# Hash attention before an MLP mixer: scores on four 32-row tiles instead of two 64-row tiles

## The chip, the core and the metric

The kernel runs on one core of one Trainium2 chip. The metric is the device time of one execution in microseconds (us). TensorE is called PE, its weight loads PEld, VectorE DVE, ScalarE ACT, GpSimd POOL; SP is the sync engine, which here only issues DMAs.

## What is computed

Attention over 4 batches of 8 heads, 768 positions, 64 columns a head, with a hash mask, and then an MLP mixer on its output (the change doesn't touch the mixer). The attention, cut to its core:

```python
q_bits = (np.einsum('bhsd,dk->bhsk', q, proj) > 0)     # 6 bits a position
k_bits = (np.einsum('bhsd,dk->bhsk', k, proj) > 0)
mask = q_bucket[:, :, :, None] == k_bucket[:, :, None, :]   # all 6 bits equal
scores = np.where(mask, scale * (q @ k.T), -1e9)
attn = exp(scores - max) ; attn = attn / (attn.sum(-1) + 1e-09)
out = attn @ v
```

The kernel adds the mask as a product of bits: each bit is +0.5 or -0.5, those of k are scaled by 2^20, and a seventh row cancels the sum where all six agree; elsewhere the exponential becomes 0. A tiny constant, 2^-70, stands in each sum and in the sum of v, so that a row with no match stays finite.

## The kernel before, in words

The 32 heads are worked in 16 pairs. A pair `n` has q and k as one tile `qk` of 128 rows: the 64 columns of head 0 above those of head 1, fp32, 768 positions each. Its work:

- **Scores** (`Half.scores`, line 356). The 768 query positions go in two halves of 384, the 768 keys in six blocks of 128, so there are 12 blocks. For a block, the two heads' products run as two matmuls of 64 rows, on the upper and lower 64 rows of the array, into two PSUM banks (one bank pair, tag `sc`). The mask follows as two bf16 matmuls of 64 rows from `bits` (7 rows are used). An fp32 matmul appears in the trace as two PE instructions.
- **Exponential** (line 363): one ACT instruction a block, 128 x 768, into a tile `e` (12 buffers).
- **Sum over keys**: DVE adds a half's six `e` into `esd` (lines 391, 395, 398); a product with ones (line 434) sums over the 128 rows, ACT takes Ln and Exp (438, 439) and DVE and ACT refine and spread it (`newton`). This is done for the pair before, one pair late.
- **Hash of the next pair** (`hashes`, line 301): four matmuls of 32 output rows; DVE makes bits (305), ACT scales them (309), and eight DMAs from SP copy them to their rows in `bits` (line 314), of which there are two, one for even and one for odd pairs.
- **Product with v** (`weigh`, line 410): 24 matmuls a half, each of 32 output rows; ACT adds the sum of v and writes `num` (416); DVE multiplies by the reciprocal (459). The sum of v came from a load of v transposed (`vT`, line 282) and an ACT activation with accumulation (289).
- Beside it DVE and ACT convert 64-bit weights (lines 177 to 206), and every second pair DVE transposes finished blocks and SP writes them out (`bounce`, 238).

PSUM has eight banks: three bank pairs `sc` (which also serve the hash and the second `acc`), one bank `sm` for sums and one bank `acc`. All engines work in the order in which the code is written (a manual schedule); SP issues its DMAs in one queue in that order. The lines that set the order of a pair:

```python
for now in halves:
    now.scores()
    ...
if before:
    before.sums()
if 0 < n < len(pairs) - 1:
    hashes(n + 1)
halves[1].add_last()
...
load_qk(n + 2)
...
halves[0].weigh()
...
halves[1].weigh()
```

Of the kernel before, what the change touches and what calls it, by code (L numbers as in the profile page):

```python
# [48 lines left out]
def kernel(  # L49
    ctx: ExitStack,  # L50
    tc: tile.TileContext,
    qk: bass.AP,
    v: bass.AP,
    vT: bass.AP,
# [8 lines left out]
    nc = tc.nc  # L63
# [14 lines left out]
    assert S == 6 * P and DM == 512 and NB <= 8 and DTOK % P == 0 and DCH % P == 0  # L78
# [14 lines left out]
    projs = const.tile([P, P + 32], F32, name="projs")  # L93
    nc.scalar.dma_start(out=projs, in_=proj_pair)
    projwide, projblk = projs[:, :P], projs[:, P:]
    ones = const.tile([P, D], F32, name="ones")
# [17 lines left out]
    nc.gpsimd.memset(bitscale, BIG)  # L114
    for j in range(4):
        if j % 2 == 0:
            nc.gpsimd.memset(bitscale[32 * j : 32 * j + 32], 1.0)
        else:
            for i in range(2):
                cancel(bitscale, 32 * j + 16 * i + NB)  # L120
# [137 lines left out]
    def attention(pool, psum, W1, W2, x0):  # L258
        bitrows = [pool.tile([P, 2, S], BF16, name=f"bits{n}", tag=f"bits{n}", bufs=1) for n in range(2)]
        loaded = {}  # L260

        def load_qk(n):
            if n >= len(pairs):
                return
            b, hp = pairs[n]
            t = pool.tile([P, 2, S], F32, name="qk", tag="qk", bufs=3)
            if n:
                nc.sync.dma_start(out=t, in_=qk[b, hp])
            else:
                for i in (1, 0):  # L270
                    nc.sync.dma_start(out=t[:, i, :HALF], in_=qk[b, hp, :, i, :HALF])
                nc.sync.dma_start(out=t[:, :, HALF:], in_=qk[b, hp, :, :, HALF:])
            loaded[n] = [t, None, None, None]

        def load_v(n):
            if n >= len(pairs):
                return
            b, hp = pairs[n]
            vn = pool.tile([P, 2, NR, D], F32, name="vn", tag="vn", bufs=2)
            nc.sync.dma_start(out=vn, in_=v[b, hp])  # L280
            vt = pool.tile([P, S], F32, name="vt", tag="vt", bufs=2)
            nc.sync.dma_start(out=vt, in_=vT[b, hp])
            loaded[n][1:3] = vn, vt

        def add_values(n):

            vt = loaded[n][2]
            vsum = pool.tile([P, 1], F32, name="vsum", tag="vsum", bufs=4)
            nc.scalar.activation(vt, vt, ACT.Copy, scale=-EPS, accum_out=vsum)
            loaded[n][3] = vsum  # L290

        def hashes(n):

            g = pool.tile([P, HALF], BF16, name="g", tag="g", bufs=2)
            if n == 1:
                ps = psum.tile([P, 512], F32, name="hp", tag="sm", bufs=1)
            else:
                ps = psum.tile([P, 2, 512], F32, name="hp", tag="sc", bufs=3)[:, 0]
            for j in range(4):
                sl = slice(HALF * (j // 2), HALF * (j // 2) + HALF)  # L300
                nc.tensor.matmul(  # L301
                    ps[32 * j : 32 * j + 32, :HALF], projblk, loaded[n][0][:, j % 2, sl],
                    start=True, stop=True,
                )
            nc.vector.tensor_scalar(g, ps[:, :HALF], 0.0, 0.5, op0=ALU.is_gt, op1=ALU.subtract)
            if n == 1:
                nc.vector.tensor_scalar(g, g, bitscale, None, op0=ALU.mult)
            else:
                nc.scalar.mul(g, g, bitscale)
            for j in range(4):  # L310
                sl = slice(HALF * (j // 2), HALF * (j // 2) + HALF)
                for i in range(2):
                    at = 32 * j + 16 * i
                    nc.sync.dma_start(
                        out=bitrows[n % 2][D * i : D * i + NB + 1, j % 2, sl], in_=g[at : at + NB + 1],
                    )

        def first_hashes(half):

            sl = slice(HALF * half, HALF * half + HALF)  # L320
            ps = psum.tile([P, 512], F32, name="hw", tag="sm" if half else "acc", bufs=1)[:, :HALF]
            for i in range(2):
                for which in (1, 0):
                    at = D * i + 32 * (1 - which)
                    nc.tensor.matmul(  # L325
                        ps[at : at + 32], projwide[:, D * i : D * i + 32], loaded[0][0][:, which, sl],
                        start=True, stop=True,
                    )
            q, k = (bitrows[0][:, which, sl] for which in range(2))
            nc.vector.tensor_scalar(k, ps, 0.0, 0.5, op0=ALU.is_gt, op1=ALU.subtract)  # L330
            if half:
                nc.vector.tensor_scalar(k, k, widescale, None, op0=ALU.mult)
            else:
                nc.scalar.mul(k, k, widescale)
            for i in range(2):
                at = D * i
                nc.vector.tensor_scalar(
                    q[at : at + 32], ps[at + 32 : at + 64], 0.0, 0.5, op0=ALU.is_gt, op1=ALU.subtract,
                )

        class Half:
# [5 lines left out]
            def scores(self):  # L347

                qkt, bits = loaded[self.n][0], bitrows[self.n % 2]
                qs = slice(HALF * self.half, HALF * self.half + HALF)  # L350
                first = self.n == self.half == 0
# [9 lines left out]
                def exponential(sc):  # L361
                    e = pool.tile([P, 2, HALF], F32, name="e", tag="e", bufs=12)
                    nc.scalar.activation(e, sc[:, :, :HALF], ACT.Exp, scale=SCALE)  # L363
                    self.es.append(e)

# [3 lines left out]
                for c in range(NR):  # L369
                    sc = psum.tile([P, 2, 512], F32, name="sc", tag="sc", bufs=3)  # L370
                    if c == self.half == 0 and not first:
                        product(sc, bits, c, True)
                        product(sc, qkt, c, False)
                        exponential(sc)
                        continue
# [4 lines left out]
                    for block, ps in waiting:  # L380
                        product(ps, bits, block, False)
                        exponential(ps)
# [17 lines left out]
            def weigh(self):  # L400

                _, vn, _, vsum = loaded[self.n]
                if self.half:
                    acc = psum.tile([P, 2, 512], F32, name="acc", tag="sc", bufs=3)[:, 0, :HALF]
                else:
                    acc = psum.tile([P, 512], F32, name="acc", tag="acc", bufs=1)[:, :HALF]
                for c, e in enumerate(self.es):
# [6 lines left out]
                if self.half == 0:  # L414
                    nums[self.n] = pool.tile([P, 2, HALF], F32, name="num", tag="num", bufs=2)
                nc.scalar.activation(  # L416
                    nums[self.n][:, self.half], acc, ACT.Identity, scale=-1.0, bias=vsum,
                )

        nums = {}  # L420

        class Quotients:
# [5 lines left out]
            def sums(self):  # L428

                ps = psum.tile([P, 512], F32, name="sums", tag="sm", bufs=1)[:, :HALF]  # L430
                for i in range(2):
                    for h in range(2):
                        at = 32 * (2 * i + h)
                        nc.tensor.matmul(  # L434
                            ps[at : at + 32], ones[:, :32], self.halves[h].d[:, i], start=True, stop=True,
                        )
# [5 lines left out]
            def newton(self):  # L442

                ps, near = self.ps, self.near
                t = pool.tile([P, HALF], F32, name="t", tag="t", bufs=1)
                rec = self.rec = pool.tile([P, 2, HALF], F32, name="rec", tag="rec", bufs=2)
                nc.vector.tensor_tensor(t, ps, near, op=ALU.mult)
# [19 lines left out]
        nc.vector.memset(bitrows[0][:, 0], 0.0)  # L467
        nc.gpsimd.memset(bitrows[1], 0.0)
        load_qk(1)

        idle = psum.tile([P, 512], F32, name="idle", tag="sm", bufs=1)
        for _ in range(6):
            zeros = bitrows[0][:, 0]
            nc.tensor.matmul(idle[:D, :HALF], zeros[:, :D], zeros[:, :HALF], start=True, stop=True)  # L474
# [9 lines left out]
        for n in range(len(pairs)):  # L484
# [3 lines left out]
            for now in halves:  # L488
                now.scores()
                if n == 0 and now.half:  # L490
                    hashes(1)
                now.add()
                if now.half == 0:
                    now.add_last()
            if before:
                before.sums()
            if 0 < n < len(pairs) - 1:
                hashes(n + 1)
# [4 lines left out]
            add_values(n)  # L503
# [4 lines left out]
            halves[0].weigh()  # L508
            if n + 1 == len(pairs):
                before.divide()  # L510
                before = Quotients(halves)
                before.sums()
                before.newton()
                weights.turnover()
                halves[1].weigh()
# [4 lines left out]
            halves[1].weigh()  # L520
# [1249 lines left out]
```

## Time and profile before

| | |
|---|---|
| median of 3 runs | 787.82 us (787.6 to 788.1) |
| span of the profiled execution | 786.3 us, 1.5 below the median |
| busy: PE, PEld, DVE, ACT, POOL | 99%, 61%, 85%, 62%, 7% |
| granted PE clock | 1.00 throughout |
| attention | from the start to about 310 us |

The span runs from the first to the last instruction of one profiled execution. In a timeline each row has the start and the length in us, engine, line, operation, the tile written and those read, shapes, and how many instructions were merged; in brackets, how long the engine was idle before and what released it. The names are those of the code, without buffer numbers.

### The profile page before, as it was taken

How to read it: one execution, taken by the hardware profiler on the slowest of the kernel's cores; microseconds unless marked ns; L12 is line 12 of the kernel's file. 1: busy time of each engine (PE TensorE's matmuls, PEld its weight loads, DVE VectorE, ACT ScalarE, POOL GpSimd, SP SyncE). 2: the span in 40 equal slices, each digit the busy share in tenths (PEclk: the TensorE clock that was granted, in tenths of full speed). 3: DMA queues.
4: the chain of work that ended last, by engine and by line, in shares of the span. 5: the costliest groups of instructions: out<-in, count | busy, mean ns of one | idle time of the engine just before them, and what ended most of it. 6: DMA issues, size and time to landing. Idle time of an engine off the chain costs nothing.

```text
span 786.3 us, 12638 instructions
## 1 busy us (share of the span) xinstructions
PE 780.1 (99%) x4751; PEld 483.5 (61%) x4751; DVE 669.5 (85%) x918; ACT 484.7 (62%) x837; POOL 54.2 (7%) x77
## 2 busy tenths in 40 slices
PE   9999999999999999999999999999999999999997
PEld 4444444444444444455544448888887888886886
DVE  5989898989897677999787888999899799889884
ACT  6688888888888887233323225656774667665331
POOL 1000000000000000011120110120000122000001
PEclk9999999999999999999999999999999999999999
DMA  4435353537352425786487897797776784850565
GB/s 165 163 125 163 125 164 125 163 124 244 125 166 88 127 95 180 200 259 133 90 253 263 276 392 276 226 295 204 233 223 203 249 251 126 242 171 2 184 170 133
DMA packets 102529, 145.38 MB, mean 185 GB/s; under 512 B 30200, under 2 KB 72640, under 8 KB 102464
## 3 DMA queue, kind: packets, MB, share of 16 engines
q1 hardware_dynamic: 94448, 119.68, 46.5%
q0 software_dynamic: 7728, 24.64, 13.5%
q8 instruction: 38, 0.62, 0.3%
q10 hardware_dynamic: 288, 0.21, 0.1%
q14 instruction: 27, 0.22, 0.1%
HBM read 101.53 MB, written 35.52 MB: 174 GB/s over the span
## 4 chain that ended last, share of the span: by engine, by line
PE 99%; DVE 0%; issue 0%; DVEq 0%
PE b L785 50%; PE sc L356 20%; PE acc L410 16%; PE t L658 5%; PE t L698 5%; PE sums L434 2%; PE hp L301 1%; PE hw L325 0%; PE idle L474 0%; DVE second L1030 0%; DVE bits L467 0%; DVE ones L97 0%; PE b L1614 0%; DVEq L1765 0%
## 5 line engine op out<-in xcount | busy, mean ns | idle before, releaser
L363 ACT ACTIVATE e<-sc 128x768 f32<-128x768 f32 x192 | 154.5, 810 | 7.0 <-PE sc L356 6.6
L356 PE MATMUL sc<-qk 64*128 64x384 f32 x768 | 153.7, 486 | 0.0
L785 PE MATMUL b<-R,second 128*128 128x256 f32 (+1 forms) x522 | 131.9, 409 | 0.0
L410 PE MATMUL acc<-e,vn 128*32 128x384 f32 x1536 | 127.0, 486 | 0.0
L785 PEld LDWEIGHTS b<-R,second 128*128 128x128 f32 x522 | 99.0, 190 | 28.7 <-issue 16.5
L395 DVE TENSOR_TENSOR esd<-esd,e 128x768 f32<-128x768 f32 x96 | 92.0, 958 | 10.4 <-ACT e L363 0.5
L410 PEld LDWEIGHTS acc<-e,vn 128*32 128x32 f32 x1536 | 49.9, 110 | 73.9 <-issue 73.5
L356 PEld LDWEIGHTS sc<-qk 64*128 64x128 f32 x768 | 68.7, 189 | 42.3 <-issue 38.1
L791 ACT COPY c<-b 128x256 f32<-128x256 f32 (+1 forms) x96 | 40.3, 426 | 79.4 <-PE b L785 68.2
L356 PE MATMUL sc<-bits 64*128 64x384 bf16 x384 | 62.5, 323 | 0.0
L785 PE MATMUL b<-XT,WC 128*128 128x256 f32 (+1 forms) x208 | 61.0, 428 | 0.0
L391 DVE SCALAR_TENSOR_TENSOR esd<-e 128x768 f32<-128x768 f32 x32 | 30.6, 955 | 23.4 <-ACT e L363 23.3
L785 PEld LDWEIGHTS b<-XT,WC 128*128 128x128 f32 x208 | 39.5, 190 | 15.4 <-issue 10.5
L785 PE MATMUL b<-XT,SW 128*128 128x256 f32 (+1 forms) x164 | 47.0, 410 | 0.0
L658 PE MATMUL t<-x,W 128*128 128x512 f32 x96 | 41.8, 593 | 0.0
L356 PEld LDWEIGHTS <-bits 64*128 64x128 bf16 x384 | 18.7, 94 | 33.1 <-issue 9.9
L416 ACT ACTIVATE num<-acc,vsum 128x384 f32<-128x384 f32 x32 | 18.6, 581 | 29.8 <-PE acc L410 29.4
L785 PEld LDWEIGHTS b<-XT,SW 128*128 128x128 f32 x164 | 31.1, 190 | 9.4 <-issue 4.1
L718 POOL DMA_DIRECT2D XT<-second x8 | 9.8, 1228 | 385.6 <-DVE second L717 363.4
L455 ACT COPY rec<-rec 32x384 f32<-32x384 f32 x64 | 32.7, 510 | 5.0 <-DVE rec L449 4.2
L398 DVE TENSOR_TENSOR esd<-esd,e 128x768 f32<-128x768 f32 x32 | 30.5, 954 | 1.9
L658 PEld LDWEIGHTS t<-x,W 128*128 128x128 f32 x96 | 18.2, 190 | 22.7 <-issue 21.3
(246 smaller groups left out, 1282.2 us busy)
## 6 DMA issues: line engine op xcount, KB each, us to landing
second<-left SPq DMA_DIRECT2D x20, 768.0 KB
raw<-in_moe_w_ch SPq DMA_DIRECT2D x16, 768.0 KB
qk<-in_qk SPq DMA_DIRECT2D x15, 768.0 KB
second<-left SPq DMA_DIRECT2D x18, 576.0 KB
seen<-in_qk POOLq DMA_DIRECT2D x21, 384.0 KB, 4.6
WC<-hidden_left SPq DMA_DIRECT2D x18, 448.0 KB
vn<-in_v SPq DMA_DIRECT2D x16, 384.0 KB
vt<-in_vT SPq DMA_DIRECT2D x16, 384.0 KB
```

The source lines that it names most:

```text
L356: nc.tensor.matmul(sc[:, i, :HALF], t[rows, 1, P * c : P * c + P], t[rows, 0, qs], start=start, stop=not start,)
L363: nc.scalar.activation(e, sc[:, :, :HALF], ACT.Exp, scale=SCALE)
L391: nc.vector.scalar_tensor_tensor(self.d, es[0], NR * EPS, es[1], op0=ALU.add, op1=ALU.add,)
L395: nc.vector.tensor_tensor(self.d, self.d, e, op=ALU.add)
L398: nc.vector.tensor_tensor(self.d, self.d, self.es[-1], op=ALU.add)
L410: nc.tensor.matmul(acc[D * i + d : D * i + d + 32], vn[:, i, c, d : d + 32], e[:, i], start=(c == 0), stop=(c == NR - 1),)
L416: nc.scalar.activation(nums[self.n][:, self.half], acc, ACT.Identity, scale=-1.0, bias=vsum,)
L455: nc.scalar.copy(rec[other : other + 32, h], rec[at : at + 32, h])
L658: nc.tensor.matmul(ps, W1[:, r, P * j : P * j + P], x[:, r], start=(r == 0), stop=(r == NR - 1),)
L698: nc.tensor.matmul(ps[at], left, right, start=start, stop=True, skip_group_check=True,)
L785: nc.tensor.matmul(ps, left(k), right(k), start=start and k == ks[0], stop=stop and k == ks[-1], skip_group_check=True,)
L791: nc.scalar.copy(c, ps)
```

## The change

Every score product is cut into two parts of 32 rows. The host lays q and k out anew (`in_qk_rows`): rows 0 to 31 and 32 to 63 serve the even key blocks of head 0 and head 1, rows 64 to 95 and 96 to 127 the odd blocks. A row group holds its 32 columns of q for all 768 positions and of k for its three blocks (384 positions), once for each of two parts, so the tile has 2 x (768 + 384) columns. `bits` has the same four row groups. Block `j` runs on the two row groups of its parity, and its second part is written in the order behind the mask product of block `j + 1`.

```diff
+        def scores(halves):
+            qkt, bits = parts(loaded[halves[0].n][0]), bitrows[halves[0].n % 2]
+            blocks = [(now, c) for now in halves for c in range(NR)]
...
+            def product(j, part):
...
+                q, k = (bits[:, :S], bits[:, S:]) if part < 0 else qkt[part]
+                qs = slice(HALF * now.half, HALF * now.half + HALF)
+                ks = slice(P * (c // 2), P * (c // 2) + P)
+                for i in range(2):
+                    at = 32 * (2 * (c % 2) + i)
+                    nc.tensor.matmul(
+                        made[j][:, i, :HALF], k[at : at + 32, ks], q[at : at + 32, qs],
+                        start=part < 0, stop=part == 1,
+                    )
+            product(0, -1)
+            for j, (now, _) in enumerate(blocks):
+                product(j, 0)
+                product(j + 1, -1)
+                product(j, 1)
+                now.exponential(made[j])
```

The hash takes six matmuls, DVE's operation becomes two (one for k on 64 rows and 192 columns, one for q on 64 rows and 384), ACT scales k's part alone, and the bits go to four row groups:

```diff
-            for j in range(4):
-                sl = slice(HALF * (j // 2), HALF * (j // 2) + HALF)
-                for i in range(2):
-                    at = 32 * j + 16 * i
+            for j in range(2):
+                for i in range(4):
+                    at, of = 32 * i, 32 * j + 8 * i
                     nc.sync.dma_start(
-                        out=bitrows[n % 2][D * i : D * i + NB + 1, j % 2, sl], in_=g[at : at + NB + 1],
+                        out=to[at : at + NB + 1, S:][:, quarter[j]], in_=g[of : of + NB + 1, : HALF // 2],
                     )
+            for j in range(2):
+                for i in range(4):
+                    at, of = 32 * i, D + 32 * j + 8 * (i % 2)
+                    nc.sync.dma_start(out=to[at : at + NB + 1, half[j]], in_=g[of : of + NB + 1])
```

All eight banks become four bank pairs in one rotation (`bank_pair`): twelve for the blocks of a pair, one that sums and hash share, one for both halves of the product with v. The exponentials go to one tile `exps` with a column of -2^-70 behind each 384, and the first half's product with v takes that column too, which gives the sum of v; the load of `vT` and its activation go.

```diff
+        exps = pool.tile([P, 2 * NR, 2, HALF + 1], F32, name="exps", tag="exps", bufs=1)
...
+        def bank_pair(name):
+            return psum.tile([P, 2, 512], F32, name=name, tag="sc", bufs=4)
...
+                columns = HALF if self.half else HALF + 1
+                acc = to[:, self.half, :columns]
...
+                    vsum = loaded[self.n][2] = pool.tile([P, 1], F32, name="vsum", tag="vsum", bufs=2)
+                    nc.scalar.copy(vsum, acc[:, HALF:])
...
-            nc.scalar.activation(vt, vt, ACT.Copy, scale=-EPS, accum_out=vsum)
```

The first pair keeps its 64-row products (`first_scores`), with its bits in a place borrowed from `x0`. In a later pair both halves' scores come first, and then the hash, the additions in the order of before, and the sums.

Where the instructions stand now. On SP, in one pair between two loads of v, before (`bits` are the copies of hash bits, `qk` the load for the pair after next, `raw` a weight, `bounced` finished output):

```order
L280 DMA vn<-in_v 128x768
L282 DMA vt<-in_vT 128x768
L314 DMA bits_136<-g 7x384 x8
L268 DMA qk<-in_qk 128x1536
L169 DMA raw<-in_moe_w_ch 128x1536
L238 DMA bounced_104<-stage 32x24x64 x4
```

and in the changed kernel:

```order
L288 DMA vn<-in_v 128x768
L319 DMA bits_147<-g 7x192 x8
L325 DMA bits_147<-g 7x384 x8
L270 DMA qk<-in_qk_rows 128x2304
L166 DMA raw<-in_moe_w_ch 128x1536
L235 DMA bounced_115<-stage 32x24x64 x4
```

Eight copies of bits became sixteen, first the eight of k with 192 columns, then the eight of q with 384, and the load of `qk` stands behind all of them.

On PE, where a pair ends with its product with v and the next pair's first blocks begin, before (`acc` is the product with v, `sc` a block; a bf16 weight load has its own row):

```order
L410 MATMUL acc<-e,vn 32x384 x48
L356 LDWEIGHTS bits_136
L356 MATMUL sc<-bits_136 128x384
L356 LDWEIGHTS bits_136
L356 MATMUL sc<-bits_136 128x384
L356 MATMUL sc<-qk 128x384 x4
```

and now, with what an instruction waits for in brackets (a DMAHW name is the landing of a DMA, here copies of bits):

```order
L442 LDWEIGHTS bits_147 [waits DMAHW0_49]
L442 MATMUL sc<-bits_147 128x384 [waits PE_49]
L442 LDWEIGHTS bits_147 [waits DMAHW1_49]
L442 MATMUL sc<-bits_147 128x384 [waits DMAHW1_49]
L442 MATMUL sc<-qk 128x384 x2
L442 LDWEIGHTS bits_147 [waits DMAHW2_49]
L442 MATMUL sc<-bits_147 128x384 [waits PE_49]
L442 LDWEIGHTS bits_147 [waits DMAHW3_49]
L442 MATMUL sc<-bits_147 128x384 [waits DMAHW3_49]
L442 MATMUL sc<-qk 128x384 x4
```

The second block's mask product, with its own two waits for bits, stands between the two halves of the first block's product. Before, the first block's mask and whole product followed each other.

More of the change, by code (lines that the diff above doesn't have):

```diff
@@ L305, in hashes @@
[L305 to L312, printed above, removed]
-                    at = 32 * j + 16 * i
+                nc.scalar.mul(g[:D, : HALF // 2], g[:D, : HALF // 2], bitscale[:D])
@@ L369, in scores @@
                 for c in range(NR):
[L370 to L375, printed above, removed]
+                    sc = bank_pair("sc")
                     product(sc, qkt, c, True)
@@ L398, in add_last, with weigh @@
                 nc.vector.tensor_tensor(self.d, self.d, self.es[-1], op=ALU.add)
[L400 to L407, printed above, removed]
+            def weigh(self, to):
+                _, vn, vsum = loaded[self.n]
+                columns = HALF if self.half else HALF + 1
+                acc = to[:, self.half, :columns]
+                for c in range(NR):
+                    e = exps[:, NR * self.half + c, :, :columns]
                     for i in range(2):
@@ L519, in attention @@
             weights.turnover()
[L520 removed]
+            halves[1].weigh(acc)
             if n and n % 2 == 0:
```

172 lines of the change are left out of this document (106 added, 66 removed).

## The prediction, made before the changed kernel ran

> **What bounds the kernel now.** I read the page first, then the busy time by stretches, then the timeline of one head pair, engine by engine. Of the page, the span, the first engine row and the chain of work that ended last:
>
> ```profile
> span 786.3 us, 12638 instructions
> PE 780.1 (99%) x4751; PEld 483.5 (61%) x4751; DVE 669.5 (85%) x918; ACT 484.7 (62%) x837; POOL 54.2 (7%) x77
> PE 99%; DVE 0%; issue 0%; DVEq 0%
> PE b L785 50%; PE sc L356 20%; PE acc L410 16%; PE t L658 5%; PE t L698 5%; PE sums L434 2%; PE hp L301 1%; PE hw L325 0%; PE idle L474 0%; DVE second L1030 0%; DVE bits L467 0%; DVE ones L97 0%; PE b L1614 0%; DVEq L1765 0%
> ```
>
> PE is busy 780.1 of 786.3 us. The change touches only the attention, lines 356, 410, 434 and 301: some 39% of the chain, the first 310 us. Its second pair begins, one in the middle runs, and the last one begins and makes its last block (timeline, PE; start and length in us, last the number of merged instructions):
>
> ```profile
> 26.02 0.34 PE L356 MATMUL sc<-bits 64*128 64x384 bf16 x2
> ...
> 109.80 0.33 PE L356 MATMUL sc<-bits 64*128 64x384 bf16 x2
> 109.96 0.81 PE L356 MATMUL sc<-qk 64*128 64x384 f32 x4
> 110.60 0.33 PE L356 MATMUL sc<-bits 64*128 64x384 bf16 x2
> ...
> 111.67 0.85 PE L434 MATMUL sums<-esd,ones 128*32 128x384 f32 x8
> 112.33 0.83 PE L301 MATMUL hp<-qk,projs 128*32 128x384 f32 x8
> 112.98 7.92 PE L410 MATMUL acc<-e,vn 128*32 128x384 f32 x96
> 120.84 0.34 PE L356 MATMUL sc<-bits 64*128 64x384 bf16 x2
> ...
> 291.51 0.34 PE L356 MATMUL sc<-bits 64*128 64x384 bf16 x2
> ...
> 301.04 0.33 PE L356 MATMUL sc<-bits 64*128 64x384 bf16 x2
> ```
>
> From 26.02 to 291.51 are 14 pairs: 18.96 us each. One pair is 12 score blocks of 0.81 us (109.80 to 110.60), sums 0.66, hash 0.65, and the product with v, 112.98 to 120.84, 7.86. ScalarE in the same pair, all engines' busy time in it (the row of sums of windows from 101.87 to 120.84), VectorE and the SP queue:
>
> ```profile
> 102.90 9.68 ACT L363 ACTIVATE e<-sc 128x768 f32<-128x768 f32 x12 [0.32 <-PE sc L356]
> 112.59 0.49 ACT L438 ACTIVATE near<-sums 128x384 f32<-128x384 f32 x1
> 113.11 0.53 ACT L439 ACTIVATE near<-near 128x384 f32<-128x384 f32 x1
> 114.31 0.62 ACT L309 ACTIVATE g<-g,bitscale 128x384 bf16<-128x384 bf16 x1 [0.68 <-DVE g L305]
> 114.84 0.83 ACT L289 ACTIVATE vt<-vt 128x768 f32<-128x768 f32 x1
> 121.87 0.81 ACT L363 ACTIVATE e<-sc 128x768 f32<-128x768 f32 x1 [0.32 <-PE sc L356]
> ```
>
> ```profile
> sum 18.97, PE 18.97 PEld 8.88 DVE 17.79 ACT 16.17 POOL 0.00; mean PE 6.32 PEld 2.96 DVE 5.93 ACT 5.39 POOL 0.00
> ```
>
> ```profile
> 104.55 0.96 DVE L391 SCALAR_TENSOR_TENSOR esd<-e 128x768 f32<-128x768 f32 x1 [0.34 <-ACT e L363]
> ...
> 113.73 0.55 DVE L305 TENSOR_SCALAR g<-hp 128x384 bf16<-128x384 f32 x1
> ```
>
> ```profile
> 104.23 4.67 SPq L238 DMA_DIRECT2D bounced<-stage  x4
> ...
> 114.96 5.91 SPq L314 DMA_DIRECT2D bits<-g  x8
> 120.91 0.44 SPq L268 DMA_DIRECT2D qk<-in_qk  x1
> 121.40 0.42 SPq L169 DMA_DIRECT2D raw<-in_moe_w_ch  x1
> ```
>
> Call E the start of a pair's first exponential; PE began that pair 1.03 us before (120.84 against 121.87). The exponentials run without a gap at 0.807 us, as fast as PE makes blocks. The next pair's hash bits are ready late: VectorE takes them at E + 10.83 (113.73 - 102.90), behind nine additions of exponentials; ScalarE scales them; SP issues the first copy of bits at G = E + 12.06. The first block of the next pair needs copies 0 to 3. The eight copies start 0.746 us apart ((5.91 - 0.69) / 7, with 0.689 us for each by this view of line 314):
>
> ```profile
> L314 SPq DMA_DIRECT2D bits<-g x120: 688/689/938, 19.4 to 291.0; - x120
> ```
>
> How soon they land is in the moved bytes, here 40 slices of 0.25 us from 112 to 122 us:
>
> ```profile
> GB/s 307 418 442 320 111 61 0 0 0 0 0 33 0 0 0 0 0 22 0 0 22 0 0 22 0 0 87 0 0 22 0 0 22 0 0 22 0 0 22 49
> ```
>
> The eight marks of 22 are the eight copies, the first in 116.25 to 116.50: at most 1.5 us after its issue began, and I take 1.3. Copy 3 lands at G + 3.5 = E + 15.6; the next scores start at E + 17.94. So the bits have 2.4 us to spare now, no wait shows, and PE alone sets the 18.96.
>
> **The change, part by part.** *Scores.* The fp32 product of a block is cut in two halves of 32 rows, and the mask product shrinks to 32 rows. A matmul of 384 columns takes as long with 64 rows as with 128:
>
> ```profile
> L356 PE MATMUL sc<-qk 64*128 64x384 f32 x768 | 153.7, 486 | 0.0
> L410 PE MATMUL acc<-e,vn 128*32 128x384 f32 x1536 | 127.0, 486 | 0.0
> L356 PE MATMUL sc<-bits 64*128 64x384 bf16 x384 | 62.5, 323 | 0.0
> ```
>
> so fewer rows save nothing; only work side by side does. The 486 and 323 hold some 0.16 us of pipeline (a block of two fp32 passes and a mask is 0.807, that is 0.323 + 0.323 + 0.161). A block on its own rows will take 4 x 0.323 + 0.161 = 1.45 us, and with even and odd blocks side by side PE makes one per 0.73 us, 0.08 less than now: 1.0 us a pair at best. That tiles on all four row groups run side by side no row of before shows. Bounds: 0.73, or 1.45 where they don't overlap. I take 0.73, because the two row tiles of now (four instructions of 0.81 us together, each listed with 0.486) and the four column tiles (96 of 0.486 in 7.92) do overlap. Yet almost nothing of it reaches the end. ScalarE still needs 0.807 a block, and with four bank pairs exponential 7 must end (E + 6.46) before block 11 starts, which then takes 1.45: PE leaves the scores at E + 8.0 instead of E + 8.7 (last mask product at 301.04 of a pair that began at 291.51). And the first block, alone on its rows, is ready 1.45 + 0.25 = 1.7 us after PE begins the pair, not 1.03. Minus 0.7 and plus 0.7: with nothing else in the way a round would be 8.0 + 0.66 + 0.65 + 7.86 + 0.1 for the change of tiles + 1.7 = 18.97 us, against 18.96.
>
> *Sum of v.* One more column in 24 matmuls, and a copy of 128x1 on ScalarE, for the activation of 0.83 us on line 289. It stands where ScalarE waits for PE anyway: nothing. The loads stay at 1,536 KB (qk grows by 384 KB, vT goes).
>
> *Hash bits.* This is where I see the price. VectorE's operation becomes two; ScalarE's takes 64x192, which no row shows. Bounds for the first part of VectorE 0.3 to 0.55 us, for ScalarE's 0.2 to 0.62; I take 0.35 and 0.42, some two thirds of now for half the columns, so G comes at E + 11.65. PE's hash work keeps 0.65 (its longest column tile still has 384 columns in all), and it ends before VectorE has made its nine additions. Then **SP issues 16 copies where it issued 8**, the eight of k first, the eight of q after. The first block of the next pair reads copies 0, 1, 8 and 9; the second 2, 3, 10 and 11. In PE's order the second block's mask product stands ahead of the first block's second half, and an instruction that waits on PE holds all behind it: nothing of the next pair is finished before copy 11 has landed.
>
> A copy of 7 rows of 384 bytes is not in the trace. Nearest rows: 0.746 for 7 rows of 768 bytes on the same queue; 0.42 to 0.44 for loads of 128 rows (121.40 and 120.91), for which bytes make no difference (6,144 a row); 1.17 for the writes of line 238 (4.67 / 4). I take 0.746, the same rows and queue. For the landing, bounds from the start of the issue are its own 0.69 us and the 2.9 of the projection load below (0.84 to 3.72); I take the 1.3 of the copies' own row.
>
> ```profile
> 0.84 0.39 ACTq L94 DMA_DIRECT2D projs<-in_proj_pair  x1
> 3.72 0.18 PEld L325 LDWEIGHTS hw<-qk,projs 128*32 128x32 f32 x2 [0.76 <-DMA projs<-in_proj_pair]
> ```
>
> Copy 11 begins at G + 11 x 0.746 = G + 8.2 and lands at G + 9.5. Then block 0's second half, 0.65, and the pipeline with a semaphore, 0.25: the next E is G + 10.4. **The new round is 11.65 + 10.4 = 22.05 us**, 3.09 over 18.96. PE would be ready at E + 17.3 and waits some 3 us a pair (copy 9 lands at E + 19.7, copy 11 at E + 21.2). VectorE (17.8 us of work, 0.35 more now), ScalarE (16.2, 1.0 less) and SP (11.9 for copies, 4.7 + 0.4 + 0.4 and a load of v) all fit in 22. The load of qk, queued behind the copies, now begins at G + 11.9 and is first read at G + 19.2; at 400 GB/s (the row of bytes) 1,152 KB need 3 us. Copies 12 and 13, which block 6 reads, land by G + 11; its bank pair is free at G + 12.8.
>
> *Sum.* The first copies go out at 19.4 now and some 0.3 later then, so the second pair's E moves from 27.05 to 30.1: +3.1. Fourteen rounds of +3.09: +43.3. The last pair's scores end 0.7 earlier: -0.7. Together **+45.7**, on the profiled 786.3 us of span 832.0; the median stands 1.5 us over the span, so about **834 us**.
>
> **Rivals.** *The bits arrive in time.* The round is then the 18.97 us worked out above, and with the shorter end of the last pair the time **787 us**: not slower, within 0.2%. For it speaks that SP has room: sixteen copies are 11.9 us of a round of 19. It decides at the step of one copy: copy 11 at E + 11.65 + 11s + 1.3 must be there when the first half of block 0 ends, at E + 18.1, so s must be 0.46 us or less, for k and q alike. Against it: the q copies have the very shape that takes 0.746. If PE's lead were worth more than I give it (12 x 0.08 = 1.0 us a pair), it would end at 773. *Only k's copies are cheap*, 0.47 us (0.42 and a gap of 0.05): copy 11 begins at 8 x 0.47 + 3 x 0.746 = 6.0, the round is 19.85, 15 x 0.9 = +13: **801 us**, still slower. *The tiles don't run side by side*, so that the change doesn't do what it says: if PE starts matmuls strictly in order, a matmul's second pass begins before the next matmul's first, and a block costs 4 x 0.323 = 1.29 us. Exponential 10 then ends at E + 13.7 (10 x 1.29 + 0.81), and with the last addition (0.96), the hash and its scaling G moves to E + 15.6; the round is 26: 15 x 7, with a last pair longer by some 5: **898 us**. Against it: by that order a step of four matmuls on line 410 would take 1.29 too, and 12 steps take 7.86, 0.655 each. [...]
>
> **How the numbers follow.** Forecast 834, chance 0.73: its own range, with the landing between its bounds (-0.6 and +1.6 us in 15 rounds), is 825 to 858. Cheap k copies, 801: 0.08. In time, 773 to 790: 0.12, of which 0.06 is faster by over 0.2%, 0.05 within 0.2% (about what a measurement of this kernel can tell from no change) and 0.01 slower. Strict order, 898, or k copies at 1.17 us (8 x 0.42 us later, 15 rounds, 884): 0.07. The range of 8 in 10 runs from 799 to 856: it takes in the first two. Faster 0.06, same 0.05, slower 0.73 + 0.08 + 0.07 + 0.01 = 0.89.
>
> **What the profile will show.** Right: SP's copies 16 to a pair, about 0.75 us apart; PE idle at each pair's first mask product, released by a DMA of bits; exponentials in a row of 12 with 22 us from row to row; G at E + 11.6. Score blocks at 0.73 us where nothing gates them would confirm the tiles. Wrong, if copies of k take under 0.5 us, if the first block goes on without copy 11, or if blocks take 1.3 us.

## The result, and the profile after

| | before | after |
|---|---|---|
| median | 787.71 us (4 runs, 787.38 to 788.1) | 865.83 us (4 runs, 864.55 to 868.8) |
| ratio | | 1.0997, 95% interval 1.0977 to 1.1017 |
| span of the profiled execution | 786.3 us | 864.5 us |
| mean granted PE clock (share of full speed) | 1.00 | 0.97 |

Slower, as forecast, but by 78 us where 46 were forecast, and outside the range of 799 to 856. Of the page of after, the span, the first engine row, the PE clock over 40 slices, the chain of work that ended last, and the costliest group:

```profile
span 864.5 us, 14288 instructions
...
PE 800.4 (93%) x5531; PEld 517.5 (60%) x5531; DVE 677.5 (78%) x933; ACT 457.7 (53%) x821; POOL 54.8 (6%) x82
...
PEclk9999999999999998999999999999999999999999
...
PE 67%; ACT 15%; DVE 9%; SPq 4%; DMA 2%; issue 2%; DVEq 0%
...
L413 PE MATMUL acc<-exps,vn 128*32 128x384 f32 (+1 forms) x1536 | 151.9, 551 | 44.7 <-ACT num L421 44.7
```

PE no longer holds the whole chain: ACT and DVE have 24% of it. The product with v (line 413, before line 410) has 44.7 us of idle time ahead of it, all ended by ACT's `num` (line 421), and one of its matmuls takes 551 ns where it took 486. One pair of after on PE (timeline; most rows of blocks are left out; the sums come first and the hash behind them, both in the tile `hash` now):

```profile
151.12 1.51 PE L442 MATMUL sc<-qk 32*128 32x384 f32 x14
152.41 0.32 PE L442 MATMUL sc<-bits 32*128 32x384 bf16 x2
...
153.87 0.32 PE L442 MATMUL sc<-bits 32*128 32x384 bf16 x2
...
155.32 0.32 PE L442 MATMUL sc<-bits 32*128 32x384 bf16 x2
...
158.70 0.85 PE L468 MATMUL hash<-esd,ones 128*32 128x384 f32 x8
160.38 0.35 PE L298 MATMUL hash<-qk,projs 128*32 128x192 f32 x1 [0.83 <-ACT near L472]
...
161.06 4.06 PE L413 MATMUL acc<-exps,vn 128*32 128x385 f32 x48
168.03 5.45 PE L413 MATMUL acc<-exps,vn 128*32 128x384 f32 x48 [2.91 <-ACT num L421]
173.41 0.35 PE L442 MATMUL sc<-bits 32*128 32x384 bf16 x4
```

The same pair on ACT (timeline of after):

```profile
151.17 8.78 ACT L358 ACTIVATE exps<-sc 128x768 f32<-128x768 f32 x12 [0.95 <-PE sc L442]
...
165.04 2.14 ACT L489 COPY rec<-rec 32x384 f32<-32x384 f32 x4 [1.32 <-DVE rec L483]
167.21 0.16 ACT L420 COPY vsum<-acc 128x1 f32<-128x1 f32 x1
167.40 0.58 ACT L421 ACTIVATE num<-acc,vsum 128x384 f32<-128x384 f32 x1
...
175.09 1.51 ACT L358 ACTIVATE exps<-sc 128x768 f32<-128x768 f32 x2 [0.95 <-PE sc L442]
```

and on SP, the sixteen copies of bits:

```profile
162.76 5.90 SPq L319 DMA_DIRECT2D bits<-g  x8
168.76 5.83 SPq L325 DMA_DIRECT2D bits<-g  x8
```

A round is 175.09 - 151.17 = 23.92 us. The copies are where the prediction put them: the first at E + 11.6, sixteen of them some 0.74 us apart. But PE hardly waits for them: it comes to the next pair's masks at 173.41. It stands still earlier, **between the two halves of its product with v**. Both halves write one tile now, the bank pair `acc`. The second half does not begin until ACT has read the first half out as `num`; `num` stands in ACT's order behind four copies of `rec`, and these wait for DVE. Before, the halves had banks of their own, and this order on ACT cost nothing.

The round by stages, from PE's rows (before: those of the prediction): scores 158.70 - (173.41 - 23.92) = 9.21 (before 9.79), sums 0.85 (0.66), wait for Ln 0.83 (none), hash 0.68 (0.65), first half with v 4.06, wait for `num` 2.91 (none), second half 173.41 - 168.03 = 5.38 (both halves before 7.86). The differences add up to -0.58 + 0.19 + 0.83 + 0.03 + 2.91 + 1.58 = +4.96, and 23.92 - 18.96 is 4.96.

The 1.58 is mostly PE's clock. By stretches of 3.41 us (PEclk is the granted clock as a share of full speed):

```profile
core 0: us, PE busy (x) PEld busy (x) DVE busy (x) ACT busy (x) POOL busy (x), PEclk, DMA share, GB/s
143.53:146.94 3.41, 2.84 (x20) 0.99 (x24) 2.77 (x4) 0.52 (x1) 0.00 (x0) 0.50 0.04 10
160.60:164.02 3.42, 3.42 (x52) 1.51 (x48) 3.22 (x6) 1.73 (x3) 0.00 (x0) 1.00 0.01 2
164.02:167.43 3.41, 1.10 (x16) 0.20 (x8) 3.31 (x6) 2.23 (x6) 0.00 (x0) 1.00 0.02 4
167.43:170.84 3.41, 2.81 (x20) 0.99 (x24) 3.38 (x5) 0.55 (x1) 0.00 (x0) 0.50 0.02 4
170.84:174.25 3.41, 3.41 (x46) 1.54 (x42) 1.17 (x2) 0.58 (x1) 0.00 (x0) 1.00 0.06 12
```

The stretch that holds the wait (PE busy 1.10 of 3.41 us) is followed by one at a granted clock of 0.50, and there the second half begins. The next such stretch before it is 143.53 to 146.94, one round earlier.

### The profile page after: what moved, and what is told of

It reads as the page before. It is cut to its first block, busy times and chain, and to the rows that moved or that the text cites. A ratio compares the mean times of both kernels' runs of the same rounds, so it can differ in the third digit from the quotient of the medians.

```text
span 864.5 us, 14288 instructions
## 1 busy us (share of the span) xinstructions
PE 800.4 (93%) x5531; PEld 517.5 (60%) x5531; DVE 677.5 (78%) x933; ACT 457.7 (53%) x821; POOL 54.8 (6%) x82
## 4 chain that ended last, share of the span: by engine, by line
PE 67%; ACT 15%; DVE 9%; SPq 4%; DMA 2%; issue 2%; DVEq 0%
PE b L828 46%; ACT exps L358 11%; PE acc L413 8%; PE t L701 5%; PE t L741 4%; PE sc L442 3%; ACT rec L489 2%; SPq L325 2%; DVE rec L483 2%; DMA bounced<-stage 2%; DVE g L308 2%; DVE esd L402 2%; DVE esd L399 1%; PE sc L370 1%; SPq L235 1%
## 5 line engine op out<-in xcount | busy, mean ns | idle before, releaser
L413 PE MATMUL acc<-exps,vn 128*32 128x384 f32 (+1 forms) x1536 | 151.9, 551 | 44.7 <-ACT num L421 44.7
L358 ACT ACTIVATE exps<-sc 128x768 f32<-128x768 f32 x192 | 141.2, 809 | 17.8 <-PE sc L442 16.4
L442 PE MATMUL sc<-qk 32*128 32x384 f32 x1440 | 137.6, 485 | 0.0
L413 PEld LDWEIGHTS acc<-exps,vn 128*32 128x32 f32 x1536 | 53.4, 122 | 137.1 <-issue 80.2
L442 PEld LDWEIGHTS sc<-qk 32*128 32x128 f32 x1440 | 104.1, 185 | 20.6 <-issue 1.7
L395 DVE SCALAR_TENSOR_TENSOR esd<-exps 128x768 f32<-128x768 f32 x32 | 30.5, 954 | 89.5 <-ACT exps L358 89.5
L399 DVE TENSOR_TENSOR esd<-esd,exps 128x768 f32<-128x768 f32 x96 | 92.0, 958 | 10.0
L442 PE MATMUL sc<-bits 32*128 32x384 bf16 x360 | 53.1, 323 | 1.3 <-DMA bits<-g 1.3
L828 PEld LDWEIGHTS b<-XT,WC 128*128 128x128 f32 x208 | 39.5, 190 | 15.4 <-issue 10.8
L402 DVE TENSOR_TENSOR esd<-esd,exps 128x768 f32<-128x768 f32 x32 | 30.7, 958 | 2.7 <-ACT exps L358 0.5
L828 PE MATMUL b<-TA,WC 128*128 128x256 f32 (+1 forms) x84 | 28.2, 440 | 0.0
```

Source lines behind the costliest of these rows:

```text
L395: nc.vector.scalar_tensor_tensor(self.d, es[0], NR * EPS, es[1], op0=ALU.add, op1=ALU.add,)
L399: nc.vector.tensor_tensor(self.d, self.d, e, op=ALU.add)
L402: nc.vector.tensor_tensor(self.d, self.d, self.es[-1], op=ALU.add)
L413: nc.tensor.matmul(acc[D * i + d : D * i + d + 32], vn[:, i, c, d : d + 32], e[:, i], start=(c == 0), stop=(c == NR - 1),)
L442: nc.tensor.matmul(made[j][:, i, :HALF], k[at : at + 32, ks], q[at : at + 32, qs], start=part < 0, stop=part == 1,)
L828: nc.tensor.matmul(ps, left(k), right(k), start=start and k == ks[0], stop=stop and k == ks[-1], skip_group_check=True,)
```

## The experiments

The theory after this reading: three new waits (for `num`, for Ln, for bits), and PE's clock at half after a long wait. The rival is the prediction's own: the sixteen copies set the round.

**1. Each half of the product with v gets a bank pair of its own** (label split_acc).

```diff
-            acc = bank_pair("acc")
-            halves[0].weigh(acc)
+            halves[0].weigh(bank_pair("acc"))
...
-            halves[1].weigh(acc)
+            halves[1].weigh(bank_pair("acc"))
```

> The changed kernel, with a bank pair of its own for each half of the product with v (15 pairs of the rotation a head pair instead of 14), so that the second half no longer stands behind ScalarE's reading of the first. Theory A (the shared pair is what holds PE): the 2.9 us wait of line 413 is gone, the next limit is the sixteen copies of bits, whose round the forecast gave as 22.05 us: about 835 us, 834 to 850 if the clock still falls. Theory B (the copies of bits already set the round of 23.9 us): no change, 866. Theory C (the half-clock windows alone are to blame, whatever opens the gap): the gap only moves to the start of the scores, 855 to 866.

Measured 866.44 us, ratio 1.0998 (1.0966 to 1.103): no gain at all. The wait for `num` is gone, and another stands in its place (timeline of this kernel, PE; the first row is the whole product with v, the others are the next pair's first blocks):

```profile
163.41 7.94 PE L413 MATMUL acc<-exps,vn 128*32 128x385 f32 x96
...
172.56 0.33 PE L442 MATMUL sc<-bits 32*128 32x384 bf16 x1 [1.21 <-DMA bits<-g]
173.29 0.32 PE L442 MATMUL sc<-bits 32*128 32x384 bf16 x1 [0.40 <-DMA bits<-g]
...
174.75 0.32 PE L442 MATMUL sc<-bits 32*128 32x384 bf16 x1 [0.38 <-DMA bits<-g]
174.76 1.37 PE L442 MATMUL sc<-qk 32*128 32x384 f32 x8
```

This is the wait that was forecast. Its copies began at 164.72 (k) and 170.73 (q); copy 11 began at 170.73 + 3 x 0.735 = 172.93, and its mask started at 174.75, 1.8 us later. The next exponential came at 176.07, so E' = G + 11.35, not + 10.4. The stretch behind the wait is at half clock (columns as above), and the pair's first blocks fall into it:

```profile
172.50:175.10 2.60, 1.76 (x12) 0.88 (x16) 1.48 (x2) 0.00 (x0) 0.00 (x0) 1.00 0.04 8
175.20:178.60 3.40, 3.40 (x28) 2.80 (x24) 0.31 (x1) 1.62 (x2) 0.00 (x0) 0.50 0.28 59
```

The gap has moved to the start of the scores, as theory C has it; that half clock alone is to blame, as C also has it, experiment 5 does not bear out. B gave the same time, but has the copies set the round of the changed kernel itself, and there PE hardly waits for them; experiment 2 tries that.

**2. The eight copies of q are issued by GpSimd** (pool_q), beside those of k on SP.

```diff
-                    nc.sync.dma_start(out=to[at : at + NB + 1, half[j]], in_=g[of : of + NB + 1])
+                    nc.gpsimd.dma_start(out=to[at : at + NB + 1, half[j]], in_=g[of : of + NB + 1])
```

> The changed kernel, with the eight copies of q's bits issued by GpSimd instead of SP, beside the eight of k. Theory A (the shared bank pair): the bits come some 3 us earlier and nothing uses that, 866 within 4 us. Theory B (the copies set the round): 800 or less. Theory C: as A.

Measured 867.65 us, ratio 1.1013 (1.0981 to 1.1045). The wait for `num` stays, 2.92 us in most pairs, 45.3 us in all where the changed kernel had 44.7 (groups by line; behind the bar the idle time ahead and its releaser):

```profile
L413 PE MATMUL acc<-exps,vn 128*32 128x384 f32 (+1 forms) x1536 | 154.6, 559 | 45.3 <-ACT num L421 45.3
```

So the copies are not what holds after, and yet each repair alone gives nothing.

**3. Both edits together** (split_acc_pool_q).

> Both edits: own bank pairs for the two halves of the product with v, and q's copies on GpSimd. Theory A with the copies next in line: PE then waits only for the Ln of the sums before the hash (0.83 us), the round is 18.97 + 0.83 = 19.8, about 800 us, clock 1.00 throughout. If split_acc alone gives the same, the copies of bits were never a limit. If there is a further limit not named yet: over 810.

Measured **796.05 us**, ratio 1.0104 (1.0075 to 1.0133), rounds of 19.43 us, the mean granted clock of the run 0.999 (0.966 and 0.968 with one of the edits alone). The two waits lie side by side, each long enough alone for rounds of some 24 us; with both away 70 of the 78 us are gone. What is left on PE is the wait for Ln, once a pair (groups by line, 20 to 300 us):

```profile
L298 PE MATMUL hash<-qk,projs 128*32 128x192 f32 x112 | 11.9, 332 | 11.6 <-ACT near L472 11.6
```

**4. The kernel before, with its set of eight copies issued twice** (before_16_copies; the second set writes the same bits again).

```diff
-            for j in range(4):
+            for j in (0, 1, 2, 3, 0, 1, 2, 3):
```

> The kernel before, with each of its eight copies of bits issued twice, a full set of eight and then the same eight again, so that the first block of the next pair needs copy 11 of sixteen. Price of the copies as in the forecast: copy 11 lands 9.5 us after the first is issued, E + 12.06 + 9.5, scores start there and the round is 22.6 instead of 18.96: 787.7 + 14 x 3.6 = 838 us, more if the clock falls in the gap of 3.6 us. If sixteen copies cost nothing that counts: 788.

Measured 877.96 us, ratio 1.1144 (1.1072 to 1.1216). Sixteen copies make the old kernel slow by themselves, with nothing else of the change (timeline, PE, the first masks of a pair):

```profile
125.86 0.50 PE L356 MATMUL sc<-bits 64*128 64x384 bf16 x1 [3.20 <-DMA bits<-g]
126.60 0.50 PE L356 MATMUL sc<-bits 64*128 64x384 bf16 x1 [0.24 <-DMA bits<-g]
126.61 2.92 PE L356 MATMUL sc<-qk 64*128 64x384 f32 x8
129.29 0.39 PE L356 MATMUL sc<-bits 64*128 64x384 bf16 x2
```

The wait is 3.2 us here and 2.8 to 4.4 in the other pairs, near what the prediction had ("some 3 us a pair"). But the rounds after the first two are 24.3 to 25.6 us, not the 22.6 expected, and the time is 878 and not 838: the products of the pair's first two blocks take 129.46 - 126.61 = 2.85 us, where two blocks took 1.6. The mean granted clock of the run is 0.963; that it was at half in these blocks is an estimate from 2.85 against 1.6.

**5. pool_q with 24 more PE instructions between the halves of the product with v** (pool_q_warm). They write the second half's bank before its own product does; nothing is left out.

```diff
+                if self.half == 0 and self.n:
+                    for _ in range(3):
+                        for i in range(2):
+                            for d in range(0, D, 32):
+                                nc.tensor.matmul(
+                                    to[D * i + d : D * i + d + 32, 1, :HALF], vn[:, i, 0, d : d + 32],
+                                    exps[:, 0, i, :HALF], start=True, stop=True,
+                                )
```

> pool_q with 12 more fp32 matmuls (24 PE instructions of 384 columns, some 2.0 us at 0.655 us per four with two passes) between the two halves of the product with v, from the second pair on. They write the second half's bank before its own product does, so the output is unchanged; they fill the time in which PE waits for num. If the idle gap costs more than itself because it makes a stretch at half clock (3.41 us in each pair), that stretch goes: clock 1.00, the second half's product 3.9 to 4.0 us instead of 5.45, round some 22.4 us instead of 24, time 838 to 846. If the half clock does not come from the gap, or the slow second half has another cause (bank, pipeline), the wait only shrinks to some 1 us, the second half stays at 5.4 and the time stays at 862 to 868.

Measured 843.48 us, ratio 1.0708 (1.0686 to 1.0729): **24 us faster than pool_q by doing more work**. Of its timeline on PE, the first half, the added work (line 421) and the second half:

```profile
151.68 4.06 PE L413 MATMUL acc<-exps,vn 128*32 128x385 f32 x48
155.56 2.12 PE L421 MATMUL acc<-exps,vn 128*32 128x384 f32 x24
158.66 4.08 PE L413 MATMUL acc<-exps,vn 128*32 128x384 f32 x48 [0.98 <-ACT num L429]
```

The second half starts as late after the first as in after (158.66 - 151.68 = 6.98 us, there 168.03 - 161.06 = 6.97), but PE's own idle part of it is 0.98 us, the second half takes 4.08 us where it took 5.45, and the mean granted clock of the run is 0.999 (0.968 in pool_q); the rounds are 22.55 us. So the slow second half comes from the idle time and not from the bank, and half clock costs about 1.4 us a round. The added work also shows what the second half waits for: it wrote the second half's bank from 155.56 on without a wait, since the halves lie in different banks of the pair and it stands ahead of `num` in the code. The second half stands behind `num` and writes the same tile; with a tile of its own (experiment 1) the wait is gone.

**6. The kernel before, with both halves of its product with v in one bank pair** (before_shared_acc).

```diff
-                if self.half:
-                    acc = psum.tile([P, 2, 512], F32, name="acc", tag="sc", bufs=3)[:, 0, :HALF]
-                else:
-                    acc = psum.tile([P, 512], F32, name="acc", tag="acc", bufs=1)[:, :HALF]
+                acc = to[:, self.half, :HALF]
...
+            acc = psum.tile([P, 2, 512], F32, name="acc", tag="sc", bufs=3)
+            halves[0].weigh(acc)
...
```

> The kernel before with one edit: both halves of the product with v write one bank pair of the rotation (tag sc) instead of two separate tiles. Its tiles, hash and 8 copies stay. If the shared bank pair alone makes the second half wait for num of the first: a wait of 2 to 3 us before the second half in each pair, and with a stretch at half clock in each pair a round of some 22 to 24 us: 825 to 866 us, clock under 0.99. If the wait comes only together with the new scores or the sum of v: 786 to 792 us.

Measured 838.06 us, ratio 1.0639 (1.0618 to 1.066): this one sharing costs the old kernel 50 us. Every pair but the first waits 1.7 to 2.4 us, but only some of them lose clock as well (0.983 in the mean of the run): after waits of 2.33 us each, the second half takes 5.77 us at 135.09 and 4.08 at 158.28. The rounds of those that lose clock are 23.2 us, the others 21.1 to 21.5. Two of these waits, both of 2.3 to 2.4 us, by stretches of 3.41 us of this kernel (columns as above):

```profile
40.64:44.05 3.41, 1.01 (x16) 0.21 (x12) 3.31 (x6) 3.20 (x6) 0.00 (x0) 1.00 0.04 10
44.05:47.46 3.41, 3.41 (x24) 1.16 (x28) 1.96 (x3) 0.00 (x0) 0.00 (x0) 0.50 0.22 49
85.01:88.42 3.41, 3.04 (x40) 1.00 (x32) 3.34 (x7) 3.05 (x6) 0.00 (x0) 1.00 0.01 3
88.42:91.83 3.41, 1.44 (x20) 0.68 (x24) 3.38 (x5) 1.86 (x4) 0.00 (x0) 1.00 0.05 12
91.83:95.24 3.41, 3.41 (x44) 1.37 (x35) 0.59 (x1) 0.58 (x1) 0.00 (x0) 1.00 0.62 199
```

Where the wait falls whole into one stretch (PE busy 1.01, idle 2.40) the next one is at 0.50; where the same wait is cut by the border of two (idle 0.37 and 1.97), the clock stays.

**7. split_acc with the copies in another order, all on SP** (split_acc_order): the first part of k (192 columns of each row group) and of q (384 positions), then the second part of both.

```diff
             for j in range(2):
                 for i in range(4):
                     at, of = 32 * i, 32 * j + 8 * i
...
-            for j in range(2):
                 for i in range(4):
                     at, of = 32 * i, D + 32 * j + 8 * (i % 2)
```

> split_acc (a bank pair of its own for each half of the product with v) with all 16 copies still on SP, but in another order: k of the first 384 columns, q of the first, k of the second, q of the second. The first block needs copies 0, 1, 4 and 5, the second 2, 3, 6 and 7, so copy 7 is the last that the start of a pair needs, not 11: it lands at G + 7 x 0.74 + 1.3 = G + 6.5, about when PE is ready. If it is the place of the copies that are needed first, and not their number, that delays the start: waits at the first mask product under 0.5 us, clock 1.00, 795 to 803 us. If their number counts (queue full, the qk load behind them late): it stays at 860 to 868. Between, 805 to 850, if the later copies (8 to 15) then delay later blocks.

Measured 826.44 us, ratio 1.0499 (1.0482 to 1.0517): between the two cases expected. The pair's first blocks no longer wait, since they need copy 7 and not copy 11. The third and fourth, whose keys reach into the second part of k, now wait for copies 8 to 11 (timeline, PE):

```profile
131.66 0.96 PE L441 MATMUL sc<-qk 32*128 32x384 f32 x8
...
133.09 0.33 PE L441 MATMUL sc<-bits 32*128 32x384 bf16 x1 [0.36 <-DMA bits<-g]
...
134.56 0.33 PE L441 MATMUL sc<-bits 32*128 32x384 bf16 x1 [0.40 <-DMA bits<-g]
```

The waits are short and lie apart, the mean granted clock of the run is 0.995 (0.966 in experiment 1), and the rounds are 20.8 to 21.7 us in all pairs after the first but one. So the place of the copies counts, but in both orders tried on one queue PE waits.

**8. split_acc_pool_q with a bank pair each for sums and hash** (split_all_pool_q).

```diff
-                hashing = bank_pair("hash")
...
-                before.sums(hashing[:, 0])
+                before.sums(bank_pair("sums")[:, 0])
...
-                hashes(n + 1, hashing[:, 1])
+                hashes(n + 1, bank_pair("hash")[:, 1])
```

> split_acc_pool_q, and sums and hash also get a bank pair each (16 of the rotation in a pair instead of 15). The hash no longer waits for Ln of the pair before it. If that wait of 0.83 us a pair is all that is left on PE: round 19.43 - 0.83 = 18.6 us, 15 x -0.83 = -12, 783 to 786 us, faster than the kernel before by some 0.4%. If the shift of the rotation makes another wait (the blocks then reach further back: a block that waits for the exponential four before it now meets num or the hash), or ScalarE sets the round: 793 to 800.

Measured 786.33 us, ratio 0.9978 (0.9966 to 0.9989); the wait for Ln is gone. The shortest rounds are 18.39 us. Where DVE also transposes output they are 19.0 to 19.6: there DVE is late with the bits, and in one pair PE waits 0.77 us for them:

```profile
193.92 0.70 PE L442 MATMUL sc<-bits 32*128 32x384 bf16 x2 [0.77 <-DMA bits<-g]
```

**9. The same, with DVE making the bits after one addition of the second half, not after three** (split_all_early).

```diff
-                for e in es[2:-1]:
-                    nc.vector.tensor_tensor(self.d, self.d, e, op=ALU.add)
+                self.more(2, 3 if self.half and self.n else NR - 1)
...
             def add_last(self):
-                nc.vector.tensor_tensor(self.d, self.d, self.es[-1], op=ALU.add)
+                self.more(3 if self.half and self.n else NR - 1, NR)
```

Here `more(first, last)` adds the exponentials from `first` up to `last`.

> split_all_pool_q, and VectorE makes the hash bits after one addition of the second half instead of after three (the two others follow behind). In split_all_pool_q the rounds are 18.4 us, but 19.0 to 19.6 where VectorE also converts a weight and transposes output: there it is late with the bits, and PE waits 0.77 us for their landing. If it is the lateness of the bits, G moves from E + 11.6 or 12.1 to some E + 10, the bits land before PE is ready in every pair, all rounds are 18.4 to 18.6, and the time 781 to 784.5 us. If VectorE's work itself (18.6 us in such a pair) or the queues set those rounds, the time stays at 785 to 787.

Measured **784.53 us**, ratio 0.9953 (0.9939 to 0.9966): 0.5% below the kernel before, a small step but clear of the interval. The copies start at E + 10.1 to 10.8 instead of E + 11.6 or later, PE waits for bits in one pair only, and the rounds after the first are 18.4 to 18.9 us but for one of 19.2. One pair of it on PE:

```profile
100.12 0.35 PE L445 MATMUL sc<-bits 32*128 32x384 bf16 x4
...
109.32 0.85 PE L471 MATMUL sums<-esd,ones 128*32 128x384 f32 x8
...
110.64 7.94 PE L416 MATMUL acc<-exps,vn 128*32 128x385 f32 x96
118.51 0.35 PE L445 MATMUL sc<-bits 32*128 32x384 bf16 x4
```

Its scores take 109.32 - 100.12 = 9.20 us against 9.79 before, and its round 18.39 against 18.96. This is what the row tiles are worth: 0.57 us a pair, where nothing else is in the way.

## Why the prediction was right or wrong

**Right: the tiles side by side.** Two blocks take 153.87 - 152.41 = 1.46 us in after, 0.73 each, as forecast. The rival of a strict order, with the two passes of a product next to each other, needed 1.29 a block: the 0.73 rules that out for tiles on different row groups, as the 0.655 of line 410 did for column groups. Whether PE starts passes out of the program's order, or the passes are interleaved already in the program, no run shows.

**Right: the hash bits and the price of a copy.** G came at E + 11.6 (162.76 - 151.17), forecast E + 11.65, and a copy with half the bytes takes the same 0.74 us. Experiment 4 shows a wait of the size that was forecast from them. The sign, slower, came out right, but in after itself for another reason than the one given.

**Wrong, and the step that failed first: "Sum", with +3.09 a round from one wait.** The working took the two halves of the product with v at 7.86 us and the hash at 0.65, as in the kernel before. The sentence on the sum of v has ACT's new copy cost nothing because "it stands where ScalarE waits for PE anyway"; what the two halves' common bank pair makes PE wait for is nowhere in the sum. It is 2.91 us a pair for `num` and 0.83 for Ln, where sums and hash share a bank pair. Both follow from the order of the code: `num` stands ahead of the second half's first matmul, Ln ahead of the hash, and each reads the tile that the later one writes.

**Wrong: a wait was priced at its own length.** Nothing in the attention of before showed what a wait does to PE's clock, since PE was idle there only at the start, 1.6 us in all. Experiment 5 puts half clock at 24 us of the 78 (867.65 - 843.48). In the kernel where the forecast wait is the one that counts (experiment 1), the round is 24.0 and not 22.05: the mask that needs copy 11 started 1.8 us after the start of that copy's issue, and the forecast had 1.3. The rest, some 1.5 us, goes with the pair's first blocks at half clock: 0.42 between that mask and the next E, and 1.04 in G, which comes at E + 12.7 (164.72 - 152.03), since that pair's twelve exponentials take 10.2 us and not 8.8. So the mechanism of the copies holds, with a cost of some 79 to 90 us where it is the wait that counts (experiments 1 and 4; in experiment 1 with 0.61 us a pair for Ln beside it); in after it is hidden behind the wait for `num`.

**Wrong: "ScalarE still needs 0.807 a block".** In after twelve exponentials take 8.78 us in a row, (8.78 - 0.81) / 11 = 0.725 each from start to start, though each is listed with 0.809. In before they started 0.807 apart because PE made blocks at that pace. So the round with nothing else in the way was 18.39 and not the 18.97 of the rival that has the bits in time, and that rival would have been the faster side of its 773 to 790: experiment 9 is there, at 784.5. The 0.25 for the pipeline with a semaphore and the 0.1 for the change of tiles in that round were the author's estimates: in after a pair's first exponential comes 175.09 - 173.41 = 1.68 us after PE begins the pair, where 1.45 + 0.25 gave 1.7; the 0.1 no run shows by itself.

Taken together, by runs: 866 (after) - 796 (experiment 3) = 70 us for the two parallel waits with the clock that goes with them, 796.05 - 786.33 = 9.7 for the wait for Ln (0.83 x 14 = 11.6 by the rows), and the rest, 786.33 - 787.84 = -1.5 us, what is left of the tiles' gain in experiment 8.

Left open: why the two waits, of different length and place, give nearly the same rounds (23.87 to 24.36 us in most pairs of after, 23.66 to 24.95 in experiment 1). In part the two lie close together: if copy 11 lets its mask go at G + 10.0, as in experiment 1, the copies would have held PE in after until 172.8 (an estimate), 0.6 us before it came to the masks. Beside that, the stretches at half clock start 23.89 us apart in after, 7 x 3.413, all but the last of the attention, and from the first of them to the last its clock changes on one grid of 3.413 us. A round without half clock is 22.5 (experiment 5), 6.6 stretches, and one with it 23.9, 7.0 stretches; a round once hit would then keep its place on the grid and be hit again (the author's estimate from these numbers). This fits, but no run moved the grid, and it may not be all: between any two stretches at half clock in the attention of after the clock stays full for 20.48 us, six of 3.413, also behind the only one of 6.83 us, where the next starts 27.31 us later.

## What to carry to other kernels

When buffers are merged into one rotation, ask of every two tiles that now share a buffer what must be read out before the second may write, and what stands ahead of that reader on its own engine: here 2.91 us a pair were lost to a reader behind five other instructions, where the change could bring 0.57. Two waits that lie side by side hide each other, so that undoing either shows nothing; undo both before calling one harmless. And an idle stretch of PE is priced with the clock that follows it: filling it with useless work gained 24 us.

## What the runs showed of the hardware

- **Half clock came after stretches of 3.413 us that were idle only in part.** In after, cut in step with the changes of its clock (from 7.00 us on, in steps of 3.413), the 14 stretches at full clock that half clock follows had 2.12 to 2.94 us of PE idle time, and no other at full clock up to 382 us had over 0.89. A stretch that was itself at half clock was followed by another after 1.01 us of idle time, and by full clock after at most 0.70. In experiment 6 a stretch with 2.40 us of idle time was followed by 0.50 and one with 1.97 by 1.00. In experiment 1 some 1.6 us were enough: in the 3.41 us before the half clock that begins at about 175.2, about 0.8 to 172.56 and 0.78 from there to 175.10 (an estimate from the timeline and the row of that stretch). In experiment 5 PE stood still for 1.34 us amid full work (134.76 to 136.10), and the clock stayed at 1.00 (130.80 to 140.20). What exactly is counted stays open.
- **An exponential that is listed with 0.81 us can start 0.71 us after the one before.** In after the first two of a pair start at 151.17 and 151.88; on average of the twelve it is 0.725, PE's own pace for a block.
- **A copy of 7 rows costs the SP queue 0.74 us whether its rows have 384 or 768 bytes** (5.90 and 5.83 us for eight), and 1.8 us pass from the start of its issue to the matmul that waits for it (experiment 1).
